# Queries and keys split in two parts: scores of the last 18 visits as float32r products of 128 rows

## The chip, the core and the metric

The kernel runs on one core of a Trainium2 chip. A core has a matrix engine (TensorE: PE is its multiplications, PEld its weight loads), a vector engine (DVE), an activation engine (ACT), a general engine (POOL), and a queue engine (SP) that here issues the DMA transfers. The metric is device time of one execution in microseconds (us); the median of three runs is shown, and one more execution was profiled. Arithmetic is on 4-byte floats. A float32r value is a float32 rounded so that TensorE can take it in one pass; a float32 product takes several.

## What is computed

Attention with a memory term over B=4 batches, H=8 heads, S=576 tokens and D=64, then two gated MLPs on the 2304 tokens of width 512:

```python
scores = scale * np.matmul(q, k.transpose(0, 1, 3, 2))       # 64 terms per score
scores = np.where(causal, -1000000000.0, scores)
a = np.exp(scores - scores.max(-1, keepdims=True))
a /= a.sum(-1, keepdims=True) + 1e-09
local = np.matmul(a, v)
q_p = np.where(q > 0, q, np.exp(q) - 1.0) + 1.0
mem_out = (q_p @ M_prev) / (q_p . z_prev + 1e-6)
x = g * mem_out + (1 - g) * local                             # g = sigmoid(beta) of the head
x = (sigmoid(x @ w_gate) * (x @ w_val)) @ w_out               # 512 -> 1536 -> 512
h = x @ w_in                                                  # 512 -> 2048
out = (h * clip(h + 3, 0, 6) / 6) @ w_out2                    # 2048 -> 512
```

## The kernel before

The program has three phases. **Phase A** computes the attention and, between its matmuls, the first part of MLP 1. **Phase B** does the rest of MLP 1, **phase C** MLP 2. The change touches phase A alone, which lasts for some 390 us of the span.

**Visits.** Attention goes through 32 visits (`VISITS`). A visit is one batch, one pair of heads and one token range: range 0 is tokens 0 to 319, range 1 is tokens 320 to 575. Per batch there are four visits of range 0 and then four of range 1, so visits 14 and 15 are the last two of range 1 of batch 1, and 16 to 31 are batches 2 and 3. `load_visit` brings queries and keys, transposed (feature by token), with head 0 of the pair in partitions 0 to 63 and head 1 in partitions 64 to 127, in a tile `qk` of two buffers; `aux` holds queries by token, values and the memory matrix.

**Scores.** `score_part` multiplies, per head, 128 queries (64 feature rows, the stationary operand) with a stretch of keys, in float32, into a PSUM tile `s`. A visit of range 0 has two parts, of 192 keys (with two small 64 by 64 products, the "ends", for the first 64 queries) and of 320; a visit of range 1 has parts of 448, 320 and 256. Each part is two matmuls, one per head, on the lower and the upper half of the array's rows. `row_max` (DVE) takes a part out of PSUM; `exponentials` (ACT), `normalize` (DVE and ACT), `transpose_bank` (tiles `t` and `T`) and `pv` follow it.

**MLP 1 in between.** `moe(fill)` issues the matmuls `m` of MLP 1 for chunks of 312 tokens: each is a float32r product of 128 rows, and each product of a weight and an activation is taken as three such matmuls, of rounded parts and remainders (`mm3`; `split` makes the two parts of an activation: ACT rounds, DVE subtracts). An attention result reaches the MLP through DRAM: `xd<-xpr`, then `xc<-xd`, then `xs`.

**Order.** On PE the program's own order holds (`manual_schedule`): in each step of `phase_a` a score part, some transposes, `pv`, and a share of `m` (`FILL`). On DVE, ACT, POOL and SP a scheduler places the instructions; every engine takes its own in order, and SP's queue likewise. PSUM tiles `s` and `m` share four buffers. Weights of the MLPs are staged by tiles `wst` (two buffers) and `wf` (one buffer), turned into float32r parts, and kept in `wslot`.

## Time and profile before

| | before |
|---|---|
| median of 3 runs | 1065.99 us (1065.2 to 1068.02) |
| profiled execution | 1065.71 us, of which the span is 1063.9 us |
| TensorE clock granted, mean | 0.996 |
| PE busy / PEld busy | 1038.0 us (98%) / 892.6 us (84%) |
| DVE / ACT / POOL busy | 648.3 us (61%) / 538.6 us (51%) / 84.2 us (8%) |
| chain that ended last | PE 89%, DVE 4%, DMA 4%, ACT 1% |

Busy shares are means over the whole span. PE ends are modelled, and consecutive matmuls overlap in the record, so the cost of a matmul is read here from one start to the next, not from its duration. The chain of waits is followed back from the last instruction to what released it each time.

### The profile page before, as it was taken

To read this page: it belongs to the slowest core of one execution; us is meant where nothing else is said; L and a number is where in the kernel's file an instruction comes from. 1 tells how busy PE (TensorE), PEld (TensorE's weight loads), DVE (VectorE), ACT (ScalarE), POOL (GpSimd) and SP (SyncE) were. 2 spreads that over 40 slices of the span, in tenths; PEclk is the share of its full clock that TensorE was granted. 3 is DMA by queue.
4 is the path that set the end of the run, shared out by engine and by line. 5 is a ranking of instruction groups with operands and counts; after the bars stand their busy time and mean duration, and the time that the engine had idled before them with its cause. 6 is when DMAs were issued, how large, how long until landed. Compare 5 with 4: busy or idle time off the path is not lost.

```text
span 1063.9 us, 16179 instructions
## 1 busy us (share of the span) xinstructions
PE 1038.0 (98%) x5904; PEld 892.6 (84%) x5904; DVE 648.3 (61%) x1549; ACT 538.6 (51%) x1165; POOL 84.2 (8%) x102
## 2 busy tenths in 40 slices
PE   6799999999999999999999999999999999999998
PEld 4467678878887899999888888888888888888886
DVE  6999755454455338888888888743454433643433
ACT  6679885566556644435444344433453433633432
POOL 2213211110111000000000000410002000000000
PEclk9899999999999999999999999999999999999999
DMA  7755642424242215337686877444414542044511
GB/s 220 223 191 184 192 126 75 137 80 124 67 126 80 64 44 180 119 119 254 228 296 246 309 259 276 158 166 177 148 30 158 218 159 99 10 168 169 218 40 59
DMA packets 66239, 164.87 MB, mean 155 GB/s; under 512 B 8432, under 2 KB 41712, under 8 KB 60272
## 3 DMA queue, kind: packets, MB, share of 16 engines
q1 hardware_dynamic: 66160, 163.85, 45.2%
q8 instruction: 46, 0.75, 0.3%
q14 instruction: 33, 0.27, 0.1%
HBM read 122.76 MB, written 41.06 MB: 154 GB/s over the span
## 4 chain that ended last, share of the span: by engine, by line
PE 89%; DVE 4%; DMA 4%; ACT 1%; SPq 1%; issue 1%; POOL 0%; ACTq 0%; DVEq 0%
PE acc L866 18%; PE pa L831 9%; PE pb L831 7%; PE m L238 6%; PE g L240 6%; PE g L238 6%; PE g L239 6%; PE m L239 5%; PE m L240 5%; PE pv L459 5%; PE t L413 4%; PE s L349 4%; PE acc L238 3%; PE acc L240 3%; PE acc L239 3%; DMA xd<-xpr 1%
## 5 line engine op out<-in xcount | busy, mean ns | idle before, releaser
L866 PE MATMUL acc<-wslot,hs 128*128 128x512 f32 x864 | 227.8, 395 | 2.2 <-ACT hs L233 2.2
L866 PEld LDWEIGHTS acc<-wslot,hs 128*128 128x128 f32 x864 | 159.5, 188 | 27.7 <-ACT hs L233 3.5
L831 PE MATMUL pa<-xq,wslot 128*128 128x384 f32 x576 | 117.3, 338 | 1.1 <-ACT u L931 0.6
L831 PEld LDWEIGHTS pa<-xq,wslot 128*128 128x128 f32 x576 | 103.7, 187 | 9.9 <-ACT u L931 0.9
L240 PE MATMUL g<-xs,wslot 128*128 128x468 f32 (+1 forms) x288 | 106.4, 370 | 0.0
L239 PE MATMUL g<-xs,wslot 128*128 128x468 f32 (+1 forms) x288 | 106.3, 369 | 0.0
L238 PE MATMUL g<-xs,wslot 128*128 128x468 f32 (+1 forms) x288 | 104.1, 369 | 0.0
L367 ACT ACTIVATE P<-P,m 128x192 f32<-128x192 f32 (+4 forms) x144 | 83.9, 585 | 28.4 <-DVE m L329 27.3
L238 PE MATMUL m<-xs,wslot 128*128 128x312 f32 x288 | 94.4, 328 | 0.4 <-ACT xs L233 0.4
L239 PE MATMUL m<-xs,wslot 128*128 128x312 f32 x288 | 88.5, 307 | 0.1
L240 PE MATMUL m<-xs,wslot 128*128 128x312 f32 x288 | 88.1, 306 | 0.0
L831 PE MATMUL pb<-xq,wslot 128*128 128x384 f32 x432 | 87.8, 338 | 0.0
L831 PEld LDWEIGHTS pb<-xq,wslot 128*128 128x128 f32 x432 | 77.9, 188 | 6.3
L349 PE MATMUL s<-qk 64*128 64x320 f32 (+3 forms) x320 | 72.5, 491 | 10.3 <-DMA qk<-in_qk 7.1
L895 DVE TENSOR_TENSOR c<-pb,u 128x384 f32<-128x384 f32 x48 | 26.6, 555 | 86.7 <-ACT u L931 85.7
L843 ACT ACTIVATE r<-c,three 128x384 f32<-128x384 f32 x72 | 44.2, 614 | 63.4 <-DVE c L895 63.4
L413 PEld LDWEIGHTS t<-ident,P 128*128 128x128 f32 x464 | 53.6, 144 | 23.2 <-issue 11.9
L234 DVE TENSOR_TENSOR hs<-r,hs 128x384 fp32r<-128x384 f32 x96 | 56.5, 593 | 26.9 <-ACT hs L233 25.4
L413 PE MATMUL t<-ident,P 128*128 128x128 f32 x464 | 67.7, 284 | 3.6 <-POOL P L382 3.5
L329 DVE CUSTOM_DVE_ANT_0 P<-s,mask 128x320 f32<-128x320 f32 (+3 forms) x144 | 62.8, 451 | 13.3 <-PE s L349 13.2
L415 ACT COPY T<-t 128x512 f32<-128x512 f32 (+2 forms) x128 | 65.9, 540 | 8.4 <-PE t L413 8.3
L157 ACT ACTIVATE wf<-wst 128x512 f32<-128x512 f32 (+1 forms) x59 | 43.9, 744 | 43.4 <-DVE wst L163 36.7
(106 smaller groups left out, 1937.9 us busy)
## 6 DMA issues: line engine op xcount, KB each, us to landing
wst<-in_wm SPq DMA_DIRECT2D x68, 512.0 KB, 5.9
wslot<-wd SPq DMA_DIRECT2D x30, 1024.0 KB, 5.1
wd<-wslot SPq DMA_DIRECT2D x16, 1024.0 KB, 4.6
wslot<-wd SPq DMA_DIRECT2D x15, 768.0 KB, 6.4
wd<-wslot SPq DMA_DIRECT2D x8, 768.0 KB, 5.8
qk<-in_qk SPq DMA_DIRECT2D x32, 160.0 KB, 2.4
aux<-in_aux SPq DMA_DIRECT2D x16, 320.0 KB, 3.8
qk<-in_qk SPq DMA_DIRECT2D x16, 288.0 KB, 3.1
```

The lines of the kernel that those rows point to most:

```text
L234: elo.tensor_tensor(lo, src, hi.bitcast(F32), op=ALU.subtract)
L238: nc.tensor.matmul(out, w[0], x[0], start=first, stop=False)
L239: nc.tensor.matmul(out, w[0], x[1], start=False, stop=False)
L240: nc.tensor.matmul(out, w[1], x[0], start=False, stop=last)
L329: self.nc.vector.tensor_tensor_reduce(out=self.row(v, rg, r, 64 + a, 64 + e), in0=ps, in1=mask, scale=-0.125, scalar=3.0e38 if a == 0 else ...
L349: nc.tensor.matmul(ps[:, : e - a], qk[rows, 0, q0 : q0 + 128], qk[rows, 1, a:e], start=True, stop=True)
L367: self.nc.scalar.activation(x, x, AF.Exp, bias=vs["m", rg][:, r : r + 1], scale=-1.0, accum_out=vs["l", rg][:, r : r + 1])
L413: nc.tensor.transpose(ps[:, 128 * n : 128 * n + 128], self.row(v, rg, r, 128 * j, 128 * j + 128), self.ident)
L415: nc.scalar.copy(pr["T", rg][:, 512 * k : 512 * k + c], ps[:, :c])
L459: nc.tensor.matmul(ps[rows, o : o + w], pr["v"][:, j, rows], T[:, c : c + w], start=(n == 0), stop=(n == last), skip_group_check=True,)
L831: nc.tensor.matmul(ps[:, :HC], w[:, i, b, cc], x[:, l, k], start=first and k == 0 and n == 0, stop=last and k == 1 and n == 2, skip_group_ ...
L866: nc.tensor.matmul(a, h[:, i, cc], w[:, l, f], start=first and f == 0 and n == 0, stop=last and f == 1 and n == 2)
```

## The change

For visits 14 to 31 (`ROUND = 14`; 8 of range 0 and 10 of range 1) the scores are computed from two parts of each operand. The host gives a further input `qkd`, in which queries and keys of one head stand twice, in partitions 0 to 63 and again in 64 to 127; `load_visit` loads one such tile per head. `split_qk` rounds both to float32r (ACT, tile `hi`, 832 columns per head in range 1 and 640 in range 0), takes the keys' remainders (DVE, tile `klo`, 576 or 320 columns), and writes the queries' remainders over the lower half of `hi` (DVE, 64 partitions, 256 or 320 columns). Per head and part, `scores` then issues two float32r matmuls of 128 rows, of the queries' rounded and remaining parts stacked, by the rounded keys and by the keys' remainders; before, it was one float32 matmul of 64 rows. The ends of range 0 stay float32, from a tile of their own that is loaded apart.

Buffers: `hi` takes the tag of the weight stage `wst`, the ends take `wf`; `ph` has one buffer instead of two; `phw` moves from a buffer of its own to the tag of `xpr`; a `qk` tile of visits before 14 is packed into 832 columns. `split_qk(v + 1)` is called in the first step of visit v, ahead of `load_visit(v + 2)`.

```diff
@@ -50,6 +50,10 @@
 
 POST = 8
 
+ROUND = 14
+
+QK = RTOK[1][1] + S
+
 FILL = (4, 9, 8, 9, 8, 8)
 
 LAG, LEAD = 1, 2
@@ -79,9 +83,9 @@
 
 
 class Kernel:
-    def __init__(self, tc, ctx, qk, aux, zz, bt, wm1, wm2, out):
+    def __init__(self, tc, ctx, qk, qkd, aux, zz, bt, wm1, wm2, out):
         self.tc, self.nc, self.ctx = tc, tc.nc, ctx
-        self.qk, self.aux, self.zz, self.bt = qk, aux, zz, bt
+        self.qk, self.qkd, self.aux, self.zz, self.bt = qk, qkd, aux, zz, bt
         self.wm1, self.wm2, self.out = wm1, wm2, out
         self.w = {}
 
@@ -254,13 +258,19 @@
         nc = self.nc
         p, ranges = VISITS[v]
         b, h = PAIRS[p]
-        qk = self.pa2.tile([128, 2, S], F32, name="qk", tag="qk")
         a = self.pa2.tile([128, 15 * D], F32, name="aux", tag="aux", bufs=3)
         rg = ranges[0]
         (t0, n), nb, j1 = RTOK[rg], len(ROWS[rg]), RANGES[rg][-1] + 1
         src = self.aux[b, h // 2]
-        nc.sync.dma_start(qk[:, 0, t0 : t0 + n], self.qk[b, h // 2, :, 0, t0 : t0 + n])
-        nc.sync.dma_start(qk[:, 1, : t0 + n], self.qk[b, h // 2, :, 1, : t0 + n])
+        if v < ROUND:
+            qk = self.pa2.tile([128, QK], F32, name="qk", tag="qk")
+            nc.sync.dma_start(qk[:, :n], self.qk[b, h // 2, :, 0, t0 : t0 + n])
+            nc.sync.dma_start(qk[:, n : t0 + 2 * n], self.qk[b, h // 2, :, 1, : t0 + n])
+        else:
+            qk = [self.pa2.tile([128, QK], F32, name="qk", tag="qk") for g in range(2)]
+            for g in range(2):
+                nc.sync.dma_start(qk[g][:, :n], self.qkd[b, h // 2, :, g, 0, t0 : t0 + n])
+                nc.sync.dma_start(qk[g][:, n : t0 + 2 * n], self.qkd[b, h // 2, :, g, 1, : t0 + n])
         q0 = 0 if rg == 0 else 5 * D
         nc.sync.dma_start(a[:, 0 : nb * D], src[:, q0 : q0 + nb * D])
         if h == 0 and rg == 0:
@@ -286,6 +296,36 @@
             "v": a[:, 5 * D :].rearrange("p (j c) -> p j c", j=5),
         }
 
+    def split_qk(self, v):
+
+
+        if not ROUND <= v < len(VISITS):
+            return
+        nc = self.nc
+        vs = self.visits[v]
+        t0, n = RTOK[vs["ranges"][0]]
+        x, w = vs["qk"], t0 + 2 * n
+        hi = self.stage.tile([128, 2, QK], F32R, name="hi", tag="wst")[:, :, :w]
+        lo = self.pa2.tile([128, 2, S], F32R, name="klo", tag="klo")[:, :, : t0 + n]
+        for g in range(2):
+            nc.scalar.copy(hi[:, g], x[g][:, :w])
+            nc.vector.tensor_tensor(lo[:, g], x[g][:, n:w], hi[:, g, n:].bitcast(F32), op=ALU.subtract)
+            q = hi[64:, g, :n]
+            nc.vector.tensor_tensor(q, x[g][64:, :n], q.bitcast(F32), op=ALU.subtract)
+        vs["hi"], vs["klo"], vs["n"] = hi, lo, (t0, n)
+        if t0 == 0:
+            b, h = vs["pair"]
+            vs["ends"] = self.stage.tile([128, 2, 64], F32, name="ends", tag="wf", bufs=1)
+            nc.sync.dma_start(vs["ends"], self.qk[b, h // 2, :, :, 0:64])
+
+    def scores(self, v, ps, g, q0, a, e):
+        nc = self.nc
+        vs = self.visits[v]
+        hi, lo, (t0, n) = vs["hi"], vs["klo"], vs["n"]
+        q = hi[:, g, q0 - t0 : q0 - t0 + 128]
+        nc.tensor.matmul(ps, q, hi[:, g, n + a : n + e], start=True, stop=False)
+        nc.tensor.matmul(ps, q, lo[:, g, a:e], start=False, stop=True)
+
     def prep_phi(self, v):
 
         if v >= len(VISITS):
@@ -294,8 +334,8 @@
         vs = self.visits[v]
         h0, rg = vs["pair"][1], vs["ranges"][0]
         nb = len(ROWS[rg])
-        ph = self.pa2.tile([128, 5, D], F32, name="ph", tag="ph")[:, :nb]
-        w = self.pa1.tile([128, 5, D], F32, name="phw", tag="phw")[:, :nb]
+        ph = self.pa2.tile([128, 5, D], F32, name="ph", tag="ph", bufs=1)[:, :nb]
+        w = self.pa2.tile([128, 5, D], F32, name="phw", tag="xpr")[:, :nb]
         nr = self.pa2.tile([128, 5], F32, name="nr", tag="nr")[:, :nb]
         flat = lambda a: a.rearrange("p r d -> p (r d)")
         qn = vs["qn"]
@@ -342,17 +382,29 @@
         nc = self.nc
         qk, rg = self.visits[v]["qk"], 0 if i < 3 else 1
         q0, off = QB[i][0], 512 - 128 * i
-        tiles = []
-        for g in range(2):
-            rows = slice(64 * g, 64 * g + 64)
-            ps = self.ps_m.tile([128, 512], F32, name="s", tag="m")
-            nc.tensor.matmul(ps[:, : e - a], qk[rows, 0, q0 : q0 + 128], qk[rows, 1, a:e], start=True, stop=True)
-            tiles.append(ps)
+        tiles = [self.ps_m.tile([128, 512], F32, name="s", tag="m") for g in range(2)]
+        if v >= ROUND:
+            for g in range(2):
+                self.scores(v, tiles[g][:, : e - a], g, q0, a, e)
+            if i == 1:
+                ends = self.visits[v]["ends"]
+        else:
+            t0, n = RTOK[rg]
+            for g in range(2):
+                rows = slice(64 * g, 64 * g + 64)
+                nc.tensor.matmul(
+                    tiles[g][:, : e - a],
+                    qk[rows, q0 - t0 : q0 - t0 + 128],
+                    qk[rows, n + a : n + e],
+                    start=True,
+                    stop=True,
+                )
+            ends = qk[:, : 2 * n].rearrange("p (t c) -> p t c", t=2)
         if i == 1:
             for g in range(2):
                 rows = slice(64 * g, 64 * g + 64)
                 nc.tensor.matmul(
-                    tiles[1][rows, e : e + 64], qk[rows, 0, 0:64], qk[rows, 1, 0:64], start=True, stop=True, skip_group_check=True
+                    tiles[1][rows, e : e + 64], ends[rows, 0, 0:64], ends[rows, 1, 0:64], start=True, stop=True, skip_group_check=True
                 )
         for g, ps in enumerate(tiles):
             self.row_max(v, rg, ROWS[rg].index((g, i)), ps[:, : e - a], a, e, self.mask[:, off + a : off + e])
@@ -629,6 +681,7 @@
                     tq += [(t + (2 if v < 4 else 3), (v, rg, j)) for j in range(len(BANKS[rg]))]
             moe(fill)
             if t < nt and i == UNITS[rg][0][-1]:
+                self.split_qk(v + 1)
                 self.load_visit(v + 2)
             if t < nt and i == RANGES[rg][-1]:
                 self.prep_phi(v + 1)
@@ -990,6 +1043,7 @@
     zz = np.concatenate([z, z[:, 0::2], z[:, 1::2]], axis=1)
     return {
         "qk": qk,
+        "qkd": np.ascontiguousarray(np.stack([qk[:, :, [64 * g + d for d in range(64)] * 2] for g in range(2)], axis=3)),
         "aux": aux,
         "zz": np.ascontiguousarray(zz),
         "bt": np.ascontiguousarray(bt.reshape(128, -1)),
```

On PE the order is the same but for the scores. In visit 23 (range 1) the first score part of 448 keys stands between matmuls `m` and the transposes `t`. Before:

```order
L239 MATMUL m_2825<-xs0_2369,wslot_1017 128x312
L240 MATMUL m_2825<-xs0_2369,wslot_1017 128x312
L349 MATMUL s_2842<-qk_2616 128x448
L349 MATMUL s_2844<-qk_2616 128x448
L413 MATMUL t_2849<-ident_94,P_2555 128x128 x4
L413 MATMUL t_2855<-ident_94,P_2555 128x128 x4
L238 MATMUL m_2825<-xs1_2374,wslot_1017 128x312
L239 MATMUL m_2825<-xs1_2374,wslot_1017 128x312
```

and now, where each `s` of one head is written by two matmuls:

```order
L243 MATMUL m_2975<-xs0_2470,wslot_1017 128x312
L244 MATMUL m_2975<-xs0_2470,wslot_1017 128x312
L326 MATMUL s_2992<-hi_2893 128x448
L327 MATMUL s_2992<-klo_2894,hi_2893 128x448
L326 MATMUL s_2993<-hi_2893 128x448
L327 MATMUL s_2993<-klo_2894,hi_2893 128x448
L465 MATMUL t_3001<-ident_94,P_2671 128x128 x4
L465 MATMUL t_3007<-ident_94,P_2671 128x128 x4
L242 MATMUL m_2975<-xs1_2475,wslot_1017 128x312
```

The two float32 matmuls became four of float32r; what stands around them did not move.

On DVE, the rows from the last two score parts of visit 14 (`P` and `m` of 320 and 256 columns; each row maximum is a pair of rows, line 329 before and 369 now) to the first part of visit 15 (448 columns). Before:

```order
L329 ISA P_1644,m_1646<-s_1743,mask_99,m_1646 128x256
L329 ISA m_1646 128x1
L329 ISA P_1644,m_1646<-s_1745,mask_99,m_1646 128x256
L329 ISA m_1646 128x1
L329 ISA P_1776,m_1778<-s_1779,mask_99 128x448
L329 ISA m_1778 128x1
L392 SCALAR_TENSOR_TENSOR l_1645<-l_1645,a1_120 128x4
L329 ISA P_1776,m_1778<-s_1781,mask_99 128x448
L329 ISA m_1778 128x1
```

and now, where lines 312 and 314 are the remainders of visit 15 (`hi_1726`, `klo_1727`), head 0 from `qk_1594` and head 1 from `qk_1595`:

```order
L312 TENSOR_TENSOR klo_1727<-qk_1594,hi_1726 128x576
L314 TENSOR_TENSOR hi_1726<-qk_1594,hi_1726 64x256
L369 ISA P_1658,m_1660<-s_1772,mask_99,m_1660 128x256
L369 ISA m_1660 128x1
L369 ISA P_1658,m_1660<-s_1773,mask_99,m_1660 128x256
L369 ISA m_1660 128x1
L369 ISA P_1807,m_1809<-s_1810,mask_99 128x448
L369 ISA m_1809 128x1
L312 TENSOR_TENSOR klo_1727<-qk_1595,hi_1726 128x576
L314 TENSOR_TENSOR hi_1726<-qk_1595,hi_1726 64x256
L238 TENSOR_TENSOR xs3_1716<-xc_1714,xs3_1716 128x312
L369 ISA P_1807,m_1809<-s_1811,mask_99 128x448
```

The remainders of head 1 of visit 15 stand behind the row maximum of head 0 of the same visit. From visit 18 on, the remainders of both heads of a visit stand behind the last row maximum of the visit two before it, and ahead of the first one of the visit between.

On SP, the transfers around the loads of `wst` that phase B uses first (`wst_4650`, `wst_4653`). Before:

```order
L499 DMA xc_1688<-xd_63 128x312
L147 DMA wst_4650<-in_wm1 128x1024 x2
L147 DMA wst_4653<-in_wm1 128x1024 x2
L265 DMA aux_1361<-in_aux 128x256
L279 DMA aux_1361<-in_aux 128x640
L473 DMA xd_63<-xpr_1493 64x320
L262 DMA qk_1473<-in_qk 128x256
L263 DMA qk_1473<-in_qk 128x576
L474 DMA xd_63<-xpr_1493 64x256
L475 DMA xd_63<-xpr_1493 64x64
L541 DMA x2p_64<-xp_1504 128x312
L499 DMA xc_1693<-xd_63 128x312
```

and now the same stretch, with the keys and queries of visit 14 (`qk_1474` and `qk_1475`, one tile per head):

```order
L593 DMA x2p_64<-xp_1507 128x312
L551 DMA xc_1709<-xd_63 128x312
L272 DMA qk_1475<-in_qkd 128x256
L273 DMA qk_1475<-in_qkd 128x576
L275 DMA aux_1473<-in_aux 128x256
L289 DMA aux_1473<-in_aux 128x640
L593 DMA x2p_64<-xp_1582 128x312
L525 DMA xd_63<-xpr_1616 64x320
L272 DMA qk_1594<-in_qkd 128x256
L273 DMA qk_1594<-in_qkd 128x576
L272 DMA qk_1595<-in_qkd 128x256
L273 DMA qk_1595<-in_qkd 128x576
```

The four loads of `wst` left this stretch; they now stand behind the last scores of phase A. The second tile of visit 14 is loaded into the buffer that the first one leaves, behind `xc_1709`.

## Rows read from the trace of the kernel before

**Rows 1.** The page: busy time by engine, and the chain's shares.

```profile
PE 1038.0 (98%) x5904; PEld 892.6 (84%) x5904; DVE 648.3 (61%) x1549; ACT 538.6 (51%) x1165; POOL 84.2 (8%) x102
PE 89%; DVE 4%; DMA 4%; ACT 1%; SPq 1%; issue 1%; POOL 0%; ACTq 0%; DVEq 0%
```

**Rows 2.** Stretches of phase A: window, length, busy by engine, clock, DMA share.

```profile
100.00:150.00 50.00, 47.86 (x311) 33.78 (x311) 35.34 (x116) 42.80 (x107) 10.70 (x13) 1.00 0.55 170
150.00:200.00 50.00, 50.00 (x377) 42.37 (x376) 27.48 (x106) 28.70 (x81) 7.57 (x13) 1.00 0.36 101
232.60:244.30 11.70, 11.70 (x81) 9.71 (x80) 7.72 (x27) 9.10 (x23) 0.80 (x2) 1.00 0.30 81
```

**Rows 3.** PE in order of time, range 1: start, duration, line, operation, count.

```profile
230.07 0.70 PE L349 MATMUL s<-qk 64*128 64x256 f32 x4
230.70 0.41 PE L238 MATMUL m<-xs,wslot 128*128 128x312 f32 x1
230.95 0.30 PE L239 MATMUL m<-xs,wslot 128*128 128x312 f32 x1
...
232.36 0.30 PE L240 MATMUL m<-xs,wslot 128*128 128x312 f32 x1
232.59 1.02 PE L349 MATMUL s<-qk 64*128 64x448 f32 x4
233.54 1.09 PE L413 MATMUL t<-ident,P 128*128 128x128 f32 x8
```

**Rows 4.** PE in order of time, range 0, and transposes behind `m`.

```profile
258.25 0.59 PE L349 MATMUL s<-qk 64*128 64x192 f32 x4
258.77 0.33 PE L354 MATMUL s<-qk 64*64 64x64 f32 x4
259.04 1.09 PE L413 MATMUL t<-ident,P 128*128 128x128 f32 x8
260.06 1.30 PE L459 MATMUL pv<-T,aux 128*64 128x256 f32 x10
...
363.58 0.30 PE L240 MATMUL m<-ha,wslot 128*128 128x312 f32 x1
363.73 1.03 PE L413 MATMUL t<-ident,P 128*128 128x128 f32 x8
364.69 1.52 PE L459 MATMUL pv<-T,aux 128*64 128x256 f32 x12
```

**Rows 5.** PE in phase C: float32r matmuls of 512 and 384 columns in turn.

```profile
818.69 1.32 PE L866 MATMUL acc<-wslot,hs 128*128 128x512 f32 x5
819.85 1.22 PE L831 MATMUL pb<-xq,wslot 128*128 128x384 f32 x6
820.91 1.32 PE L866 MATMUL acc<-wslot,hs 128*128 128x512 f32 x5
```

**Rows 6.** Groups by form: rounding on ACT and remainders on DVE; busy, mean ns.

```profile
L233 ACT CAST ha<-th 128x312 fp32r<-128x312 f32 x36 | 16.2, 451 | 23.7 <-DVE th L524 23.5
L233 ACT CAST xq<-xh 128x768 fp32r<-128x768 f32 x15 | 12.5, 832 | 3.4 <-PE pb L831 1.9 <-POOL xh L798 1.2 <-PE g L240 0.4
L234 DVE TENSOR_TENSOR xs<-xc,xs 128x312 fp32r<-128x312 f32 x24 | 11.7, 493 | 13.1 <-ACT xs L233 13.1
L234 DVE TENSOR_TENSOR xq<-xh,xq 128x768 fp32r<-128x768 f32 x15 | 15.5, 1040 | 2.7 <-ACT xq L233 2.6
```

**Rows 7.** The chain from 115 to 136 us: start, duration, link.

```profile
118.17 5.98 DMA wst<-in_wm
...
124.16 5.96 DMA xd<-xpr
```

**Rows 8.** PE there: an idle time and its releaser.

```profile
130.03 0.86 PE L459 MATMUL pv<-T,aux 128*64 128x256 f32 x6 [1.61 <-ACT T L415]
```

**Rows 9.** The page: DMA issues of `qk`, range 1, keys: KB each, us to landing.

```profile
qk<-in_qk SPq DMA_DIRECT2D x16, 288.0 KB, 3.1
```

**Rows 10.** DVE at the first row maximum of visit 15.

```profile
143.94 0.62 DVE L329 CUSTOM_DVE_ANT_0 P<-s,mask 128x448 f32<-128x448 f32 x1 [1.10 <-PE s L349]
```

## The prediction

> **What bounds the kernel now.** I read the page first: PE is busy for 98% of the span and holds 89% of the chain that ended last; ACT and DVE are at 51% and 61% [rows 1]. Those are means over three phases, so next I read stretches of phase A. From 150 to 200 us PE is busy without a gap at full clock (1.00, the 2.4 GHz level); from 100 to 150 it stands still for 2.14 us; in one whole visit of range 1, 11.70 us long, PE is full, ACT is busy for 9.10 us and DVE for 7.72 [rows 2]. So in the stretch that the change touches a microsecond taken off PE is a microsecond of the program, as long as ACT and DVE, which get more to do, stay behind PE. Last I read PE's own rows in order of time. The column of durations misleads there, so all prices below are from one start to the next.
>
> **PE: what a score part costs now.** A part is two float32 matmuls, one per head. 256 columns last from 230.07 to 230.70, 0.63 us; 448 columns from 232.59 to 233.54, 0.95 us [rows 3]. The difference, 0.32 us over 192 columns, is 1.67 ns a column, or four passes at 2.4 GHz; so 320 columns take 0.74. What is left does not grow with the columns: 0.63 - 256 x 1.67 ns = 0.20 us in each part. Around it there is more. The `m` before a part starts at 232.36 and the part at 232.59; ten `m` from 230.95 to 232.36 stand 0.141 apart, so 0.09 is lost going in. The first `m` behind a part takes from 230.70 to 230.95, which loses another 0.11 [rows 3]. Where transposes stand behind the part, eight of them last 1.02 us (259.04 to 260.06) and 0.96 behind `m` (363.73 to 364.69), so 0.06 is lost there instead [rows 4].
>
> **PE: what it costs after.** Four float32r matmuls of 128 rows stand in its place. Six of 384 columns take 1.06 us and five of 512 take 1.16, or 0.177 and 0.232 each [rows 5]: 0.43 ns a column and 0.012 fixed. By that line 312 columns should take 0.146, and the `m` above take 0.141. Then 448 columns cost 4 x 0.204 = 0.82, 320 cost 4 x 0.149 = 0.60 and 256 cost 4 x 0.122 = 0.49. For 192 the line gives 0.094, and 0.141 is a bound from the narrowest ones in the trace; I take 0.107, nearer to the line, so 0.43. The passes over the columns are thus as many as before (four for two heads at once, against four one after the other). All of the gain is the fixed loss of entering and leaving float32:
> - 448 columns: 0.09 + 0.95 + 0.06 - 0.82 = 0.28, in 10 visits: 2.8 us.
> - 320 columns: 0.09 + 0.74 + 0.06 - 0.60 = 0.29, in 18 visits: 5.2 us.
> - 256 columns, with `m` on both sides: 0.09 + 0.63 + 0.11 - 0.49 = 0.34, in 10 visits: 3.4 us.
> - 192 columns: the block of 0.52 (258.25 to 258.77) becomes 0.43. The ends stay float32, so the loss of going in stays, and the ends, 0.27 now [rows 4], pay the fixed 0.20 instead of 0.27 - 64 x 1.67 ns = 0.16. That is 0.05 a visit, in 8: 0.4 us.
>
> Together 11.8 us. With 192 columns at 0.141 it is 10.7, and without the 0.06 behind the parts 10.1; with the line's 0.094, 12.2.
>
> A rule of the Trainium skill speaks against this sum. First the row: the `m` are float32r of 128 rows, each loads its own weights, and they start 0.141 us apart [rows 3]. The page "TensorE: Matmul & The Clock Gate", Part 3, "What overlaps and what doesn't" has it that a weight load overlaps running matmuls only when its row group differs. The old parts used two row groups, the new ones use all rows each time. By this rule each new matmul would pay its load and the sum would be a loss of some 16 us (worked out as the last rival below); by the row it is the gain above. The row does not bear the rule out.
>
> **ACT and DVE: what is added.** Rounding takes ACT 451 ns for 312 columns and 832 for 768 [rows 6], 0.84 ns a column: 0.89 us for 832 columns and 0.73 for 640, twice a visit. Remainders take DVE 493 ns for 312 and 1040 for 768 [rows 6], 1.2 ns a column: 0.81 us for 576 columns, 0.50 for 320, 0.43 for 256. So a visit of range 1 adds 1.8 us of ACT and 2.5 of DVE, one of range 0 adds 1.5 and 2.0. That is 30 and 41 us in all, and it costs nothing where PE runs on beside it. In the steady order the split is made a whole visit before its scores: its buffers come free with the last part of the visit two before, and PE has a full visit of 11 us to go. In front of the row maxima of 448 columns it makes them some 2 us late, but PE comes back for those PSUM tiles several matmul groups later. The cover is thin on ACT: 9.10 + 1.8 of a visit that would then last for 10.8 [rows 2]. Transposed tiles and rounded activations would come late in such visits. I put 1.0 us on it over all (0 to 5).
>
> **Visits 14 and 15, where there is no lead.** Both tiles of a visit need a buffer each, and at the change of layout the second tile waits until the first one's split is done. For visit 15 the DVE order puts the remainders of head 1 behind the row maximum of head 0: 0.62 us (the row maximum at 143.94 [rows 10]) + 0.81 + 0.43, so PE waits 1.9 us for its second head. By the transfers it is no better: the buffer of the first tile comes free with the last part of visit 13, six `m` behind the `pv` of 130.03 [rows 8], at about 132; a load lands in 3.1 us [rows 9], its split takes 0.9 + 1.2, the second load another 3.1 and its split as much, which is about 143 to 144, while the scores, whose first row maximum now starts at 143.94, would be due at 141 to 142. I take 2.5 us (0 to 5).
>
> **The loads that leave.** Four loads of 512 KB that phase B needs stand in SP's queue at 117 us now, and the chain runs through them: `wst` 5.98 us, then `xd` 5.96 [rows 7], though a transfer of 288 KB elsewhere lands in 3.1 [rows 9]. PE idles 1.61 us there [rows 8] of the 2.14 in 100 to 150 [rows 2]. Without these loads `xd` and `xc` land sooner. What is late next is the second tile of visit 14, which is loaded behind that `xc`. I take -1.5 (-2.1 to +1.5). Issued behind the last scores instead, the four have the last transposes, `pv` and `m` of phase A to land in, and they took 5.98 us here [rows 7].
>
> **The rest.** One buffer for `ph`, and `phw` sharing with `xpr`, tie DVE to POOL and to the transfers of the visit before. Early in the program the scheduler's other order can give or take; I count 0, and bound it by the one idle time shown, 1.6 us either way. Twice the bytes for 18 visits meet DMA engines that are busy 0.36 of the time [rows 2]: 0.
>
> **Sum.** -11.8 + 1.0 + 2.5 - 1.5 = -9.8 us. Against the profiled execution, 1065.71 us, that is 1055.9. The median of the three runs is 0.3 above it, so I say 1056.
>
> **The rivals.**
> - *Narrow float32r is slow.* No float32r matmul under 312 columns is in the trace. If those of 192 ran at float32's four passes, each would take 192 x 1.67 ns = 0.32 us, four of them 1.28 instead of 0.43: 0.85 x 8 visits = 6.8 us, and the time 1062.7. For it: nothing shows the contrary. Against: the line through 312, 384 and 512 columns is straight. Were 256 columns slow as well, 4 x 0.43 - 0.49 = 1.23 in 10 visits would come on top, and the time 1075.
> - *The fixed loss belongs to every score part, not to float32.* Then only the passes change: 0.06 to 0.07 us more for each of 38 wide parts, and 0.11 for 8 narrow ones, together 3.3 us. With 2.0 from the other terms the time is 1071, slower. It decides once some 0.28 us a part remain: 46 x 0.28 = 12.9, which undoes the 9.8 and 3 more. For it: the loss is seen at each part. Against: transposes, other products with other operands, start 0.15 behind an `m` (363.58 to 363.73), as the next `m` would, and cost 0.12 each [rows 4].
> - *ACT or DVE becomes the bound.* If PE waits for the split or for what is queued behind it by 0.5 us in each of 16 visits, 8 us go, and the time is 1064. For it: ACT at 9.1 of 11.7 us. Against: the lead of a visit.
> - *Loads of weights in series.* The new matmuls use all rows, so that a load may have to wait until the matmul ahead of it is done. If that added the 0.141 us of a whole `m` to each of the 4 x 46 = 184, it would be 26 us, and the time 1082. For it: two heads no longer share the array. Against: the pitch of the `m` [rows 3].
>
> **How the numbers follow.** Forecast 0.58; narrow matmuls slow 0.16 (0.12 for 192 columns alone, 0.04 for 256 too); fixed loss stays 0.07; ACT or DVE bound 0.14; loads in series 0.03; something not thought of, slower, 0.02. A measurement of this kernel tells 0.3%, 3.2 us, from no change: faster is under 1062.8, slower above 1069.2. The forecast is faster throughout; of the narrow case half of the 0.12 is, and of the ACT case a third, about 0.05. Faster 0.69, same 0.15, slower 0.16. The forecast's own range is 1052 to 1060: the sum's bounds do not all fall on one side. The range goes on to 1067, which takes in the narrow case and that of ACT; above lie 0.16, and below 0.04.
>
> **What would show it.** Starts of `m` on either side of a 256-column part 0.14 + 0.49 + 0.14 apart, with no loss going in or out; four matmuls of 192 columns in about 0.43 (1.28: narrow is slow). One wait of PE of 2 to 3 us for `klo` in visit 15 and hardly one after it; ACT near full in visits of range 1 with no PE wait for `T` or `ha`. No `wst` in the chain from 115 to 136 us. Phases B and C as long as before. If PE shows waits for `klo`, `T` or `xs` in every visit, or if the new matmuls stand more than 0.2 us apart at 320 columns, the forecast is wrong.

## The result, and the profile after

The changed kernel takes 1078.55 us (median of 4 runs, 1078.11 to 1079.77) against 1065.68 for the kernel before (4 runs beside it, 1065.2 to 1068.02). The ratio is 1.0118, with a 95% interval of 1.0101 to 1.0136: 12.9 us slower, where 10 us faster was forecast. The page of the profiled execution, span 1075.9 us, answers to [rows 1]:

```profile
PE 1036.4 (96%) x5904; PEld 910.7 (85%) x5904; DVE 688.2 (64%) x1621; ACT 563.4 (52%) x1201; POOL 84.5 (8%) x102
PE 87%; DVE 4%; DMA 3%; ACT 2%; SPq 1%; issue 1%; POOL 0%; ACTq 0%; DVEq 0%; POOLq 0%
```

PE is busy for 1.6 us less, and idle for 13.6 us more. So PE stands somewhere, for longer than the cheaper products can give back. To find where, I took the start of the first score part of each visit from PE's rows and set it against the kernel before (positive is later, us):

| visit | 5 | 8 | 13 | 17 | 26 | 28 | 31 |
|---|---|---|---|---|---|---|---|
| the changed kernel | 7.6 | 15.4 | 15.4 | 17.1 | 12.4 | 15.0 | 12.6 |

This table shows where to look. The changed kernel is 15.4 us late at visit 8, before the first float32r score exists (visit 14). It loses another 2 around visits 13 to 17, wins 4.7 from there to visit 26, as the change means it to, loses 2.6 at visits 26 to 28, and wins again to the end. So the stretch to read is the one up to the first score part of visit 8, in which both kernels have the same work for PE. Before, with the columns of [rows 2]:

```profile
0.00:71.85 71.85, 56.89 (x349) 37.44 (x349) 58.74 (x186) 49.43 (x123) 16.86 (x29) 0.95 0.67 207
```

and the changed kernel:

```profile
0.00:87.26 87.26, 64.24 (x348) 40.66 (x349) 70.18 (x200) 55.57 (x128) 19.11 (x29) 0.84 0.61 194
```

For the same matmuls PE is idle for 23.0 us instead of 15.0, and busy for 64.2 instead of 56.9, at a granted clock of 0.84 instead of 0.95. So about half of the 15.4 us is waiting, and the other half is the lower clock at which PE then works.

**What PE waits for there.** Waits of PE from 20 to 108 us (what it waited for: us in all, times, longest), before:

```profile
PE t L413 <- POOL P L382: 3.3, 2, 2.4
PE s L349 <- DVE xpr L470: 1.4, 2, 1.0
```

and the changed kernel:

```profile
PE t L465 <- POOL P L434: 8.8, 2, 6.0
PE s L395 <- DVE xpr L522: 3.6, 1, 3.6
```

The transposes `t` wait for the memory rows that POOL writes into `P`; the scores `s` wait for a PSUM buffer that DVE's step on `xpr` has to read first. For `t`, the reason is in POOL's own order. Before (start, duration, line, operation):

```profile
27.16 0.78 POOL L306 TENSOR_TENSOR phw<-ph,zz 128x64 f32<-128x64 f32 x1 [6.59 <-DVE l L392]
27.89 0.72 POOL L310 TENSOR_TENSOR phw<-ph,zz 128x256 f32<-128x256 f32 x1
28.72 0.72 POOL L382 TENSOR_TENSOR P<-ph,nr 128x320 f32<-128x320 f32 x1
36.19 0.77 POOL L382 TENSOR_TENSOR P<-ph,nr 128x320 f32<-128x320 f32 x1 [6.75 <-PE rl L429]
```

and the changed kernel:

```profile
29.83 0.72 POOL L434 TENSOR_TENSOR P<-ph,nr 128x320 f32<-128x320 f32 x1 [6.92 <-DVE nr L446]
32.65 0.64 POOL L346 TENSOR_TENSOR phw<-ph,zz 128x64 f32<-128x64 f32 x1 [2.10 <-DVE ph L344]
33.26 0.72 POOL L350 TENSOR_TENSOR phw<-ph,zz 128x256 f32<-128x256 f32 x1
41.59 1.62 POOL L434 TENSOR_TENSOR P<-ph,nr 128x320 f32<-128x320 f32 x1 [7.61 <-DVE nr L446]
```

Before, `phw<-ph,zz` of the next visit stands ahead of the memory rows `P<-ph,nr` of this one; now it stands behind them. With one `ph`, the next visit's `ph` can't be written until POOL has read this one's. In visits 0 to 7 (`POST = 8`) those memory rows are scaled by `nr`, which already holds the sums of the softmax, so they come at the end of a visit. That makes a ring from visit to visit: sums, memory rows, next `ph`, `phw`, `nr`, next memory rows. The two memory rows are 7.5 us apart before and 11.8 after. DVE shows what the second of them waited for in the changed kernel:

```profile
35.59 0.48 DVE L351 TENSOR_REDUCE nr<-phw 128x5 f32<-128x320 f32 x1
37.12 0.16 DVE L444 SCALAR_TENSOR_TENSOR l<-l,a 128x5 f32<-128x5 f32 x1
40.62 0.18 DVE L354 RECIPROCAL nr<-nr 128x5 f32<-128x5 f32 x1
41.29 0.16 DVE L446 TENSOR_TENSOR nr<-nr,l 128x5 f32<-128x5 f32 x1
```

The sums `l` are there at 37.12; `nr`, which comes around the ring, is ready only behind 40.62, since its steps stand in DVE's queue between row maxima and weight conversions. So here the ring comes last. One visit on it is the sums that come last (50.65, against 49.44 for `nr`): the ring alone does not set the pace of every visit.

**The products themselves.** PE around a part of 256 and one of 448 keys, range 1, which answer to [rows 3]:

```profile
233.45 0.31 PE L244 MATMUL m<-xs,wslot 128*128 128x312 f32 x1
233.60 0.28 PE L326 MATMUL s<-hi 128*128 128x256 f32 x1
233.71 0.28 PE L327 MATMUL s<-klo,hi 128*128 128x256 f32 x1
...
235.77 0.37 PE L326 MATMUL s<-hi 128*128 128x448 f32 x1
235.97 0.36 PE L327 MATMUL s<-klo,hi 128*128 128x448 f32 x1
236.18 0.36 PE L326 MATMUL s<-hi 128*128 128x448 f32 x1
236.38 0.36 PE L327 MATMUL s<-klo,hi 128*128 128x448 f32 x1
236.58 1.04 PE L465 MATMUL t<-ident,P 128*128 128x128 f32 x8
```

and range 0, which answers to [rows 4]:

```profile
271.46 0.26 PE L326 MATMUL s<-hi 128*128 128x192 f32 x1
271.56 0.27 PE L327 MATMUL s<-klo,hi 128*128 128x192 f32 x1
271.67 0.27 PE L326 MATMUL s<-hi 128*128 128x192 f32 x1
271.78 0.27 PE L327 MATMUL s<-klo,hi 128*128 128x192 f32 x1
271.98 0.33 PE L406 MATMUL s<-ends 64*64 64x64 f32 x4
```

The part starts 0.15 behind the last `m`, as one more `m` would: nothing is lost going in. 256 columns stand 0.11 to 0.12 apart, 448 stand 0.20 apart, and 192, narrower than any float32r matmul before, 0.10 to 0.11. The last 192 takes 0.20 to the ends: that is the way into float32, paid there.

### The profile page after: what moved, and what is told of

It is laid out like the page before. It is cut to its first block, busy times and chain, and to the rows that moved or that the text cites. A ratio compares the mean times of both kernels' runs of the same rounds, so it can differ in the third digit from the quotient of the medians.

```text
span 1075.9 us, 16492 instructions
## 1 busy us (share of the span) xinstructions
PE 1036.4 (96%) x5904; PEld 910.7 (85%) x5904; DVE 688.2 (64%) x1621; ACT 563.4 (52%) x1201; POOL 84.5 (8%) x102
## 4 chain that ended last, share of the span: by engine, by line
PE 87%; DVE 4%; DMA 3%; ACT 2%; SPq 1%; issue 1%; POOL 0%; ACTq 0%; DVEq 0%; POOLq 0%
PE acc L919 18%; PE pa L884 9%; PE pb L884 7%; PE g L244 6%; PE g L242 6%; PE m L242 6%; PE g L243 6%; PE m L243 5%; PE m L244 5%; PE pv L511 5%; PE t L465 4%; PE acc L242 3%; PE acc L244 3%; PE acc L243 3%; PE s L395 1%; DMA aux<-in_aux 1%
## 5 line engine op out<-in xcount | busy, mean ns | idle before, releaser
L419 ACT ACTIVATE P<-P,m 128x448 f32<-128x448 f32 (+4 forms) x144 | 84.0, 585 | 14.4 <-DVE m L369 14.0
L467 ACT COPY T<-t 128x512 f32<-128x512 f32 (+2 forms) x128 | 66.0, 541 | 16.7 <-PE t L465 16.4
L465 PEld LDWEIGHTS t<-ident,P 128*128 128x128 f32 x464 | 57.5, 149 | 19.2 <-POOL P L434 10.7
L511 PE MATMUL pv<-T,aux 128*64 128x256 f32 (+2 forms) x512 | 62.7, 378 | 3.7 <-ACT T L467 3.6
```

The costliest lines, as they stand in the source:

```text
L419: self.nc.scalar.activation(x, x, AF.Exp, bias=vs["m", rg][:, r : r + 1], scale=-1.0, accum_out=vs["l", rg][:, r : r + 1])
L465: nc.tensor.transpose(ps[:, 128 * n : 128 * n + 128], self.row(v, rg, r, 128 * j, 128 * j + 128), self.ident)
L467: nc.scalar.copy(pr["T", rg][:, 512 * k : 512 * k + c], ps[:, :c])
L511: nc.tensor.matmul(ps[rows, o : o + w], pr["v"][:, j, rows], T[:, c : c + w], start=(n == 0), stop=(n == last), skip_group_check=True,)
```

## The experiments

The lateness of visits, measured as in the table above, for every run told of below (us against the kernel before). It is read from one profiled execution of each kernel, for all but the kernel before one of the runs of its median; where that execution lies far from the median, the text says so.

| visit | 5 | 8 | 13 | 17 | 26 | 28 | 31 |
|---|---|---|---|---|---|---|---|
| 1: before, both buffers shared | 7.3 | 16.4 | 17.4 | 16.1 | 16.2 | 16.3 | 16.3 |
| 2: changed, both given back | 2.4 | 4.6 | 6.6 | 8.8 | 4.5 | 7.1 | 4.7 |
| 3: changed, two `ph` | 0.3 | 1.0 | 2.6 | 7.0 | 2.6 | 3.7 | 1.2 |
| 4: changed, own `phw` | 6.5 | 10.3 | 8.6 | 10.4 | 5.5 | 8.1 | 5.7 |
| 5: before, one `ph` | 5.9 | 8.4 | 9.3 | 8.0 | 8.4 | 8.5 | 8.5 |
| 6: before, `phw` in `xpr` | 0.1 | 0.1 | 2.0 | 3.2 | 3.9 | 4.0 | 4.0 |
| 7: as 1, conversions held | 3.3 | 10.9 | 16.7 | 18.9 | 19.2 | 19.3 | 19.3 |
| 8: as 3, from visit 16 | 0.4 | 1.0 | 1.2 | 1.1 | -3.8 | -1.2 | -3.6 |
| 9: changed, two `ph` to visit 7 | -0.2 | 0.0 | 0.5 | 5.2 | 1.9 | 2.8 | 0.3 |
| 10: as 9, own `phw`, from 16 | 0.7 | -0.1 | -1.2 | -1.0 | -5.3 | -4.2 | -6.7 |
| 11: as 8, float32 products | -0.4 | -0.3 | -0.2 | 1.9 | 2.1 | 4.8 | 4.9 |
| 12: as 10, visit 28 float32 | -0.7 | -0.2 | -1.2 | -0.8 | -5.5 | -5.6 | -7.1 |

**First: is it the two buffers?** Theory A says that the loss is in the buffer edits of `prep_phi` and has nothing to do with the scores. Rival B puts it on what the float32r visits bring (their buffers, loads, the packed tile). Experiment 1 makes the two edits in the kernel before:

```diff
-        ph = self.pa2.tile([128, 5, D], F32, name="ph", tag="ph")[:, :nb]
-        w = self.pa1.tile([128, 5, D], F32, name="phw", tag="phw")[:, :nb]
+        ph = self.pa2.tile([128, 5, D], F32, name="ph", tag="ph", bufs=1)[:, :nb]
+        w = self.pa2.tile([128, 5, D], F32, name="phw", tag="xpr")[:, :nb]
```

> The kernel before with only the two buffer edits of the change: one buffer for ph, and phw in xpr's tag. No float32r scores, no split, no new input. Theory A (these two edits hold DVE up in the first 100 us and let the scheduler set weight conversions ahead of row maxima; first m of MLP 1 at 61.7 us instead of 50.9, visit 14 some 18 us late): the median is 15 to 20 us above before, 1081 to 1086, and visit 14 starts near 151 us. Rival B (the loss comes from the float32r visits' own buffers, loads and the packed qk tile): 1064 to 1068, and visit 14 starts near 133.

Measured: 1080.63 (before 1065.13), ratio 1.0132 (1.0116 to 1.0148), 15.5 us. Without a single float32r score the whole loss is there: visit 8 is 16.4 us late, and visit 14 starts at 150.5 us, near the 151 of Theory A (the median is 0.4 us below its range). Rival B falls for this part.

Experiments 2 to 4 go the other way, from the changed kernel: both edits undone, or one. In 2 `phw` lies in a tag that early visits leave free, since both do not fit otherwise.

```diff
-        ph = self.pa2.tile([128, 5, D], F32, name="ph", tag="ph", bufs=1)[:, :nb]        # 2 and 3
+        ph = self.pa2.tile([128, 5, D], F32, name="ph", tag="ph")[:, :nb]
-        w = self.pa2.tile([128, 5, D], F32, name="phw", tag="xpr")[:, :nb]               # 2
+        w = self.pa2.tile([128, 5, D], F32, name="phw", tag="klo" if v < ROUND - 1 else "xpr")[:, :nb]
-        w = self.pa2.tile([128, 5, D], F32, name="phw", tag="xpr")[:, :nb]               # 4
+        w = self.pa1.tile([128, 5, D], F32, name="phw", tag="phw")[:, :nb]
```

> The changed kernel with two buffers for ph again, and with phw out of xpr's tag for the visits before 14 (it lies in klo's tag, which those visits leave free). All of the float32r scores stay. Theory A: the early loss of some 18 us goes, the gain on PE (about 10 us) stays less 4 to 7 us of waits in visits 13 to 15 and 28: 1058 to 1063. Rival B: no different from the changed kernel, 1076 to 1080.

> The changed kernel with two buffers for ph; phw stays in xpr's tag. Theory A1 (the single ph is what holds DVE and POOL, and moves the weight conversions): most of the loss goes, 1058 to 1065. Theory A2 (phw waiting for the transfers of xpr is what costs): it stays, 1073 to 1080.

> The changed kernel with phw in a buffer of its own; ph stays single. Theory A1 (single ph costs): 1073 to 1080. Theory A2 (phw waiting for the transfers of xpr costs): 1058 to 1065.

Measured: 1068.95 for 2, ratio 1.0031 (1.0013 to 1.0049); 1067.20 for 3, 0.9999 (0.9981 to 1.0018); 1070.79 for 4, 1.0047 (1.0028 to 1.0066). By the medians two `ph` alone win back 11 us, an own `phw` alone 8, both together no more than the first. A1 holds better than A2, but the two don't add, and all three medians lie outside what I had expected. In 3 visit 8 is on time but for 1.0 us, and 5 to 6 us are lost from visit 13 to 17 and at visits 26 to 28 (below). In 2 visit 13 is still 6.6 us late, 4.6 of it at visit 8 already, and up to there PE does not wait longer: it is idle for 14.5 us, about as before the change (15.0), but busy for 61.9 instead of 56.9, at a granted clock of 0.87 instead of 0.95. Why the clock was lower there is not shown; the runs of 2 lie far apart, from 1064.3 to 1073.9.

**Second: waits, or the order that follows from them?** In the changed kernel the scheduler also sets weight conversions on DVE (`wslot<-wst`, nine in phase A) ahead of where they stood: in front of visit 8's first row maximum there are seven, five before. Theory O says that this order costs, rival W that the waits do. Experiment 5 has the first line of experiment 1, experiment 6 the second. I took each edit by itself to leave the conversions in place, so that 5 and 6 would test the waits without the order.

> The kernel before with one buffer for ph and nothing else of the change. On DVE the weight conversions then stand where they stood before. Theory O (what costs in the first 100 us is that the scheduler, with both buffers shared, sets two weight conversions more ahead of the row maxima of visits 5 to 11): 1065 to 1069. Rival W (the waits for the single ph itself cost): 1071 to 1080.

> The kernel before with phw in xpr's tag and nothing else of the change; the weight conversions stand where they stood before. Theory O: 1065 to 1069. Rival W2 (phw waiting for the transfers of xpr costs by itself): 1071 to 1080.

Measured: 1074.30, ratio 1.0088 (1.0072 to 1.0105), and 1069.29, ratio 1.0030 (1.0019 to 1.0041). Whether the conversions did stay, DVE's rows tell. Conversions done in front of the first row maximum of a visit:

| visit | 5 | 6 | 7 | 8 |
|---|---|---|---|---|
| before; 3, 6, and 8 to 12 | 2 | 2 | 3 | 5 |
| the changed kernel, 1 | 3 | 4 | 5 | 7 |
| 4, 5 | 3 | 4 | 5 | 6 |
| 2 | 2 | 2 | 4 | 6 |
| 7 | 2 | 3 | 3 | 4 |

In 6 they stayed, in 5 they did not: a single `ph` is enough to move them. Before, the third conversion stands behind the first row maximum of visit 6 (the first line here); in experiment 5 it stands ahead of that of visit 5:

```profile
49.22 0.62 DVE L329 CUSTOM_DVE_ANT_0 P<-s,mask 128x448 f32<-128x448 f32 x1
52.18 1.22 DVE L169 TENSOR_TENSOR wslot<-wst,wslot 128x1024 fp32r<-128x1024 f32 x1
...
45.17 1.22 DVE L169 TENSOR_TENSOR wslot<-wst,wslot 128x1024 fp32r<-128x1024 f32 x1
48.19 0.60 DVE L329 CUSTOM_DVE_ANT_0 P<-s,mask 128x448 f32<-128x448 f32 x1
```

So the single `ph` costs 8.8 us together with the order that the scheduler makes of it, and 5 does not refute theory O. Waits of PE in 5, from 20 to 108 us:

```profile
PE t L413 <- POOL P L382: 6.5, 2, 4.8
PE s L349 <- DVE xpr L470: 3.6, 1, 3.6
```

They are the two of the changed kernel. The longer one, 4.8 us, ends at 41.61, before the third conversion is done. Three conversion steps, 2.5 us in all, that stood behind the `nr` of this visit before the change stand in front of it now (35.33, 36.76 and 39.08 on DVE). Taking them off, I estimate that some 2.3 us of this wait are the ring's. The other, 3.6 us, ends at 54.73, behind the moved conversion, and there ring and order are not told apart. `phw` in `xpr` costs 3.8 us with the order unchanged, less than I had put against it and more than nothing. The two medians add up to 12.6 of the 15.5 us, but not in the same place: at visit 8, where experiment 1 is 16.4 us late, 5 is 8.4 late and 6 is 0.1. About half of the early loss comes only with both edits together.

Experiment 7 shares both buffers and holds the conversions back:

```diff
+            zero = self.stage.tile([128, 1], F32, name="zero", tag="zero")
+            nc.scalar.activation(zero, self.gate[:, 0:1], AF.Copy, scale=0.0)   # gate: sums of the visit before
-        nc.scalar.activation(w, hif, AF.Abs)
+            nc.scalar.activation(w, hif, AF.Abs, bias=zero[:, 0:1])
```

> Both buffers shared as in the first experiment, but from visit 5 on a weight conversion starts only when the visit before has its sums (its first step on ACT takes a zero made of them). The conversions then stand on DVE about where they stood before the change. Theory O: most of the 15 us comes back, 1066 to 1071. Rival W (the waits of the shared buffers cost, wherever the conversions stand): 1076 to 1083.

Measured: 1085.63, ratio 1.0197 (1.0180 to 1.0214), worse than without the hold, and outside both ranges. The conversions no longer stand ahead (last row of the table), and visit 8 is still 10.9 us late, where experiment 1 is 16.4. So the moved conversions may be worth some 5 us there; but the hold has a cost of its own, and from visit 11 on the weights come late and it loses more than it gave. What the order adds to the waits stays open.

**Third: in which visits does the single `ph` cost?** If the ring runs over the sums, it is there only in visits 0 to 7. Experiment 9 gives the changed kernel two buffers there and leaves one from visit 8 on:

```diff
-        ph = self.pa2.tile([128, 5, D], F32, name="ph", tag="ph", bufs=1)[:, :nb]
+        ph = (self.pa2.tile([128, 5, D], F32, name="ph", tag="klo") if v < POST else
+              self.pa2.tile([128, 5, D], F32, name="ph", tag="ph", bufs=1))[:, :nb]
```

> The changed kernel with two buffers for ph in visits 0 to 7 only (they lie in klo's tag, which is free there); from visit 8 on ph is single, and phw stays in xpr's tag. Visits 0 to 7 are those in which the memory rows wait for the sums of the softmax. If the single ph costs there alone (the next visit's phi waits for memory rows that wait for sums): as the third experiment, 1064 to 1069. If it costs as much behind visit 8: 1073 to 1079.

Measured: 1066.26, ratio 1.0006 (0.9996 to 1.0015). 12.3 of the 12.9 us are back with two buffers in eight visits, and visit 13 is 0.5 us late. From visit 8 on one `ph` costs nothing that can be measured. This settles which edit costs, and where: the single `ph` in visits 0 to 7. The conversions are back in their old places as well, so it does not say by which way.

**Fourth: the changeover.** Experiments 3 and 9 lose 4 to 5 us between visits 13 and 17, although visits 14 to 16 are to gain there. In the changed kernel ACT shows it, from 140 to 147 us:

```profile
140.22 0.56 ACT L467 COPY T<-t 128x512 f32<-128x512 f32 x1
141.83 0.89 ACT L311 CAST hi<-qk 128x832 fp32r<-128x832 f32 x1 [1.05 <-DMA qk<-in_qkd]
142.62 0.66 ACT L419 ACTIVATE P<-P,m 128x448 f32<-128x448 f32 x1
143.19 0.19 ACT L419 ACTIVATION_READ_ACCUMULATOR P<-P,m 128x1 f32 x1
143.28 2.54 ACT L453 ACTIVATE P<-P,l 128x448 f32<-128x448 f32 x4
145.73 0.93 ACT L467 COPY T<-t 128x512 f32<-128x512 f32 x2
```

and PE and its stretches there:

```profile
146.35 1.40 PE L511 MATMUL pv<-T,aux 128*64 128x320 f32 x10 [3.15 <-ACT T L467]
147.68 0.46 PE L242 MATMUL m<-ha,wslot 128*128 128x312 f32 x1
147.94 0.46 PE L243 MATMUL m<-ha,wslot 128*128 128x312 f32 x1
...
147.50:151.00 3.50, 3.50 (x15) 2.36 (x14) 1.59 (x4) 1.13 (x2) 0.00 (x0) 0.56 0.58 137
```

The rounding of visit 14's first head stands in ACT's queue, waits 1.05 us for its load and takes 0.89, and all behind it, up to the copy of `T`, is late by that; `pv` waits 3.15 us, where the kernel before waits 1.61 [rows 8]. After that wait the `m` stand 0.26 us apart instead of 0.14: the clock is granted at 0.56 from 147.5 to 151, near the 1.2 GHz level. Experiment 8 moves the changeover to visit 16, the first of range 0, whose visits are longer and whose tiles are smaller:

```diff
-ROUND = 14
+ROUND = 16
-        ph = self.pa2.tile([128, 5, D], F32, name="ph", tag="ph", bufs=1)[:, :nb]
+        ph = self.pa2.tile([128, 5, D], F32, name="ph", tag="ph")[:, :nb]
```

> The changed kernel with two buffers for ph and the float32r scores from visit 16 on instead of 14. If visits 14 and 15, which change over without lead, cost more than they give (visit 16 starts 4.8 us later against before than visit 13 in the third experiment): 1058 to 1063. If the changeover costs the same wherever it is: 1066 to 1069.

Measured: 1061.21, ratio 0.9972 (0.9957 to 0.9988). Against experiment 3 that is 6.0 us better by the medians and 3.8 by the means (their runs overlap: 1060.4 to 1068.0 and 1060.1 to 1065.2), with two visits fewer in float32r. From visit 13 to 17 nothing is lost, and it is the first version below the kernel before.

**Fifth: the products by themselves.** Experiment 11 keeps all of experiment 8 but the products:

```diff
-        nc.tensor.matmul(ps, q, hi[:, g, n + a : n + e], start=True, stop=False)
-        nc.tensor.matmul(ps, q, lo[:, g, a:e], start=False, stop=True)
+        x = hi[64 * g : 64 * g + 64, g].bitcast(F32)
+        nc.tensor.matmul(ps, x[:, q0 - t0 : q0 - t0 + 128], x[:, n + a : n + e], start=True, stop=True)
```

> The eighth experiment (float32r from visit 16 on, two ph) with all its loads, rounding and remainders, but the scores as one float32 product of 64 rows per head from the rounded tile: the remainders of the keys are left out, and head 1 takes the remainders of its queries for them. It prices the products alone. By the prediction's terms: 8 x 0.34 + 8 x 0.91 = 10.0 us more than the eighth, 1070 to 1073. If the fixed loss belongs to every score part: 1060 to 1063.

Measured: 1070.17, ratio 1.0040 (1.0026 to 1.0054), 9.0 us above experiment 8 (their runs don't overlap: 1068.2 to 1071.7 and 1060.1 to 1065.2). The float32r products of 16 visits are worth 9.0 us by the medians and 7.2 by the two ratios, 10.0 by the prediction's terms. The lateness of 11 stays at 1.9 to 2.1 from visit 17 to 26: there the whole split, a visit ahead, costs nothing.

**Sixth: visits 26 to 28, and a better version.** Experiments 8 and 11 lose 2.6 and 2.7 us there, as the changed kernel does. DVE of the changed kernel at that place:

```profile
310.49 0.75 DVE L312 TENSOR_TENSOR klo<-qk,hi 128x576 fp32r<-128x576 f32 x1
311.27 0.42 DVE L314 TENSOR_TENSOR hi<-qk,hi 64x256 fp32r<-64x256 f32 x1
311.72 0.48 DVE L576 SCALAR_TENSOR_TENSOR th<-th,m 128x312 f32<-128x312 f32 x1
...
313.92 0.44 DVE L238 TENSOR_TENSOR ha<-th,ha 128x312 fp32r<-128x312 f32 x1
```

and PE:

```profile
312.74 0.41 PE L242 MATMUL m<-ha,wslot 128*128 128x312 f32 x1 [0.94 <-ACT ha L237]
314.41 0.41 PE L243 MATMUL m<-ha,wslot 128*128 128x312 f32 x1 [1.26 <-DVE ha L238]
```

The remainders of visit 28 stand ahead of `th` and `ha`, for which PE waits at the last change of chunk. Experiment 10 puts what was learnt together: float32r from visit 16, the early `ph` of experiment 9, and `phw` in its own buffer. Experiment 12 is the same with visit 28 left in float32 (`KEEP = (28,)` beside each test of `ROUND`).

> Float32r scores from visit 16 on, two buffers for ph in visits 0 to 7 (in klo's tag), and phw in a buffer of its own. The weight conversions stand on DVE as before the change. If all that the first 100 us lost is in these two buffers: 1057 to 1061, below the eighth experiment (1061.2). If phw in xpr's tag costs nothing here: 1060 to 1063.

> The tenth experiment with visit 28 left in float32, so that no rounding or remainder stands on ACT and DVE at the last change of chunk, where visits 26 to 28 lose 1 to 3 us against before. If that split is what delays the activations of MLP 1 there: PE waits there for ha as before (0.9 us, not 2.3), visit 28 gives up 0.9 us of products, and the time is 0.5 to 2 us below the tenth, 1059 to 1062. If the loss there is not from that split: 1062 to 1064.

Measured: 1061.97, ratio 0.9963 (0.9947 to 0.9978), and 1061.32, ratio 0.9961 (0.9947 to 0.9976). In 12 the loss at visits 26 to 28 is gone (-5.5 to -5.6; one PE wait for `ha` of 0.85 us is left, as before the change, where it is 0.91), so it was the split of visit 28. By the medians 10 and 12 are the same in time. All of 8, 10 and 12 beat both kernels, by about 4 us against before, and can't be told apart. That 10 is 3 us earlier than 8 in the table and not in its median is a matter of the execution profiled: that of 10 is the quickest of its seven runs (1058.1, the others up to 1064.2), that of 12 the second of ten (1057.8, of 1057.1 to 1065.3), that of 8 lies at its median (1061.65). The granted clock goes with it: in the four quickest runs of 10 it is 0.995 to 0.997, in the three slowest 0.988 to 0.991. So an own `phw` gains nothing here that can be measured, the second case of the expectation.

## Why the prediction was wrong

- **The step that failed** is the one called "the rest": "One buffer for `ph`, and `phw` sharing with `xpr`, tie DVE to POOL and to the transfers of the visit before ... I count 0, and bound it by the one idle time shown, 1.6 us either way." The two edits cost 15.5 us in the kernel before (experiment 1), and two buffers for `ph` in visits 0 to 7 alone take back 12.3 of the 12.9 us (experiment 9). The ring could have been read in the code: with one buffer the next `ph` waits for memory rows, and for v < `POST` these wait for the sums. I bounded a new wait by the size of an old one, in a stretch where PE is not full, and never followed who waits for whom around the ring. About half of the time lost up to visit 8 is waiting and half is work at a lower clock. How the waiting divides between the ring and the conversions that the scheduler moves with it stays open; in experiment 5 some 2.3 of the longest wait, 4.8 us, are the ring's by my estimate.
- **The products** came out as worked out. A part of 448 with its transposes fell from 1.97 to 1.69 us beyond the `m` around it (0.28 forecast, 0.28 measured), 256 from 0.82 to 0.47 (0.34, 0.35), 320 in front of transposes from 1.54 to 1.24 (0.29, 0.30), 192 by 0.10 (0.05). Only 320 in front of `pv` gave 0.15, in 8 of 18 cases: the fourth product takes 0.23 there, so `pv` pays the way into float32 that the part paid before. Summed: 11.3 us against 11.8.
- **Narrow float32r is not slow** (rival, 0.16): 0.10 to 0.11 us for 192 columns. **The fixed loss** belongs to float32, not to each part, as experiment 11 shows with time. **Loads in series** (0.03) did not come either: the new matmuls of 128 rows, each with a weight load recorded at 0.19 us, stand 0.10 to 0.20 apart. The rule of the Trainium skill ("TensorE: Matmul & The Clock Gate", Part 3, "What overlaps and what doesn't") that a weight load overlaps only where row groups differ is not what these rows show.
- **ACT and DVE prices** held: 883 ns and 727 for the two roundings (0.89 and 0.73), 854 and 508 for the keys' remainders (0.81 and 0.50). That a visit's lead hides them held from visit 17 to 26. The term of 1.0 us (0 to 5) was too small at one place: 2.6 us at visits 26 to 28.
- **Visit 15** waited where it was forecast to: 1.95 us for `hi`, the last step of the split for which I had named `klo` (1.9 by DVE's order, 2.5 put on it; the sum by the transfers comes to 142.4, not to 143 to 144). What I did not see was visit 13: the split of visit 14 in ACT's queue makes the visit *before* it late, a wait of 3.15 us for 1.61 before, and the low clock behind it costs more. **The loads that leave** gave somewhat more than was put on them, though by another way: in experiments 10 and 12 visit 15 comes 2.3 us earlier against visit 12 (-1.5 forecast, -2.1 the bound), but of the 1.61 us of idle time that I had put down to these loads [rows 8] 1.11 are still there.

## What to carry to other kernels

When an edit takes a buffer away, follow the ring it closes: who reads the tile last, and whether that reader waits for the end of the stage; then look for it where the bounding engine is not yet full. An operation that is put into an in-order queue ahead of time brings its own wait along, and charges it to all that stands behind it. A gain that is right per instruction is worth testing in parts, since here moving the start by two visits and one small buffer turned 12.9 us of loss into some 4 of gain.

## What the runs showed of the hardware

- A float32 part between float32r matmuls loses about 0.09 us going in, 0.20 within and 0.11 coming out [rows 3]; a float32r part of 128 rows loses none of it (0.15 from the last `m` to the part, as to one more `m`). The columns cost about the same: 1.67 ns each in float32 for two heads at once, or four matmuls of 0.43.
- Float32r matmuls of 256, 320 and 448 columns stand 0.12, 0.15 and 0.20 us apart, on the line through 312, 384 and 512; those of 192 stand 0.11 apart, where the line gives 0.094.
- A wait of PE can cost twice: behind the one of 3.15 us the `m` run at 0.26 us apart up to 151.4, and from 314 to 318 us, behind waits of 0.94 and 1.26, the clock is granted at 0.64 (below). Not every wait does: behind the 1.61 us at 130.03 in the kernel before, the clock stays at 1.00.

```profile
314.00:318.00 4.00, 3.59 (x20) 3.30 (x21) 3.94 (x17) 1.20 (x4) 1.04 (x2) 0.64 0.72 242
```
